# Running the softmax maxima 22 steps instead of 24 ahead of the exponentials in a fused attention block

## The chip, the core and the metric

The kernel runs on one core of one Trainium2 chip. The metric is the device time of one execution in microseconds (us); lower is better. The time quoted for a kernel is the median of its runs. A profile is taken of one more execution, and its trace gives the start and end of every instruction on the five engines: TensorE (PE, with its weight loads as PEld), VectorE (DVE), ScalarE (ACT), GpSimd (POOL) and SyncE (SP, which here only issues DMAs).

## The reference

A block with adaptive layer norms around a multi-head attention and an MLP, for 2048 rows of 512 values, 32 heads of 16 values:

```python
mod = (_silu(c) @ w_mod).reshape(c.shape[0], 6, 1, -1)
sa, ca, ga, sb, cb, gb = (mod[:, 0], mod[:, 1], mod[:, 2], mod[:, 3], mod[:, 4], mod[:, 5])
h = _layernorm(x, axis=-1) * (1 + ca) + sa
x = x + ga * _A_ref(h, A_wqkv, A_wo)        # attention
h = _layernorm(x, axis=-1) * (1 + cb) + sb
x = x + gb * _B_ref(h, B_w1, B_w2, B_w3, B_w4)  # MLP with shifted rows
# inside _A_ref:
scores = jnp.einsum("bhqd,bhkd->bhqk", q, k) * (Dh ** -0.5)
p = _softmax(scores, axis=-1)
o = jnp.einsum("bhqk,bhkd->bhqd", p, v)
```

The softmax over 2048 keys is what this change concerns. It is computed as exp(score - maximum of the row), so the maximum of each query row must be known before the first exponential of that row.

## The kernel before

**Units and steps.** Attention works through 64 units. A unit is one chunk of 512 query rows (4 chunks) times one pair of heads (16 pairs); a pair of heads lies in the two halves of the 128 partitions, `j` = 0 and 1. A unit has 16 steps, one for each tile of 128 keys, so there are 1024 steps `s`. A step has two half-steps, one for each `j`.

**What a half-step does.** Scores are computed twice, in two layouts. `score_part` (L995) computes 128 keys x 512 queries with keys on the partitions into tile `sc` (PE, L1009), and ACT takes the exponential of it into `pt` (L1005). `max_part` (L977) computes 128 queries x 512 keys into tile `mb` (PE, L993), and DVE reduces it to a row maximum `mx` (L989). `row_pair` (L1011) puts a score of step `s` and a maximum of step `s + LEAD` side by side, in different halves of the PE array, so that the two matmuls overlap. `LEAD` is the constant that the change touches; before, it is 24, one and a half units.

**From the maxima to the scores.** When the 32 maxima of a unit are done (the last is a half-step with `j` = 0), `max_fin` (L1026) finishes them: a small DVE reduce over `mx` into `mf` (L1039), two small ACT instructions (L1040, L1041), a small POOL subtraction (L1042), and then `shift_rows`, eight small DMAs on SP that write the negative maxima into two extra rows for each half of the unit's query tile `qtl` (in the trace `qtl<-nm`, 8 for a unit; all DMAs carry line L132). With those rows the score matmul subtracts the maximum by itself: it reads rows `64*j` to `64*j+63` of `qtl`, while the maximum's matmul reads only the first 62 of them. So the first score matmul of a unit with `j` = 0 has to wait until the first four of the eight DMAs have landed, and the one with `j` = 1 until all eight have.

**The rest of a step.** POOL turns each `pt` into its low half (`p_low`, L1058; now and then ACT does it, L153), and the PV matmuls (L1083, L1080) follow the exponentials by `LAG` = 2 blocks. At the end of a unit ACT copies the PV sums out (`ac`, L1100), PE turns them (`ot`, L1110), and ACT, DVE and POOL finish them (L1117, L1125, L1121).

**What sets the order.** The half-steps are taken in blocks of three, and each engine's instructions are written out in the order that a planner makes when the kernel is built; at run time every engine goes through its own list in order. The planner counts its own costs and due times (`Sched`); it holds a score back for the shift rows only by the moment they are issued, without a price for eight DMAs. All score and maximum tiles share 7 PSUM banks.

```python
blocks = [list(range(i, min(i + GRP, 2 * NS))) for i in range(-2 * LEAD, 2 * NS, GRP)]
...
        if s + LEAD < NS:
            parts.append((1 - j, max_part(s + LEAD, 1 - j)))
```

**Stages.** Before the first exponential, PE makes the maxima of the first `LEAD` steps alone, between projection matmuls. In the first quarter of attention the remaining projections (tiles `k`, `q`, `v`) are fitted between the blocks (`fill`). From then on nothing but attention runs, until the MLP begins. Loads of a unit's keys and queries are issued 32 steps ahead of its scores into one of three buffers (`load_unit`, L957), those of its values 6 steps ahead (`load_v`, L966), all on SP's one queue, in the order of the program.

Of the kernel before, what the change touches and what calls it, by code (L numbers as in the profile page):

```python
# [34 lines left out]
VMAX = 2.0 ** 14  # L35
VD = 20

LEAD = 24
LAG = 2
CARRY = 3000.0  # L40
BMAX = 1600.0
# [286 lines left out]
def kernel(ctx, tc, A_x, A_wqkv, A_wo, B_w1, B_w2, B_w3, B_w4, c, w_mod, out):  # L328
# [648 lines left out]
    def max_part(m, j):  # L977

        u, i = divmod(m, 16)
        c, g = divmod(i, 4)  # L980
        if u not in mxs:
            mxs[u] = at.tile([P, 2, 4, NC], F32, name="mx", tag="mx", bufs=2)
        x, b = bank("mb")
        ready, sm.t[x] = sm.t[x], LATE
        r = slice(64 * j, 64 * j + 62)
        lhs = qst[u][r, (g // 2) * 256:(g // 2 + 1) * 256].rearrange("p (n l) -> p l n", l=2)[:, g % 2]

        def after(e):
            end = sch.crit("D", 605, e + PX, lambda: dve.reduce_max(mxs[u][:, j, g, c:c + 1], b, axis=AX.X))  # L989
            sm.t[x] = end + XP["D"]  # L990
            if (c, g, j) == (NC - 1, 3, 0):
                max_fin(u)
        return ready, lambda: te.matmul(b, lhs, kst[u % 3][r, c * CH:(c + 1) * CH], start=True, stop=True), after  # L993

    def score_part(s, j):  # L995

        u, kt = divmod(s, NKT)
        if j == 0:
            pt[s] = at.tile([P, 2, CH], I32, name="pt", tag="pt", bufs=NPT)
        x, b = bank("sc")  # L1000
        ready, sm.t[x] = sm.t[x], LATE
        r = slice(64 * j, 64 * j + 64)

        def after(e):
            ea = sch.crit("A", 480, e + PX, lambda: act.activation(pt[s][:, j], b, AF.Exp))  # L1005
            sm.t[x] = ea + XP["A"]
            if j:
                e_exp[s] = e_hi[s] = ea
        return ready, lambda: te.matmul(b, kst[u % 3][r, kt * P:(kt + 1) * P], qst[u][r], start=True, stop=True), after  # L1009

    def row_pair(s, j):  # L1011

        parts = []
        if 0 <= s < NS:
            parts.append((j, score_part(s, j)))
        if s + LEAD < NS:
            parts.append((1 - j, max_part(s + LEAD, 1 - j)))
        parts = [x for _, x in sorted(parts, key=lambda x: x[0])]
# [575 lines left out]

    blocks = [list(range(i, min(i + GRP, 2 * NS))) for i in range(-2 * LEAD, 2 * NS, GRP)]
    pvs = [x for s in range(0, NS, 2) for x in ((s, 0), (s + 1, 0), (s, 1))]
    due = 0.0
    for k, blk in enumerate(blocks + [[]] * (LAG + CPER)):
# [18 lines left out]
        t, start = CIN, 0.0  # L1617
        need = sum((s >= 0) + (s + LEAD < NS) for s, _ in row)
        sch.flush(need)
        banks = sorted(sm.t)  # L1620
        n = 0
        for s, i in row:
            n += (s >= 0) + (s + LEAD < NS)

# [102 lines left out]
```

## Time and profile before

| | before |
|---|---|
| median of 3 runs | 2030.32 us (2027.38 to 2033.31) |
| profiled execution | 2025.04 us, of which the span is 2023.3 us |
| granted TensorE clock | 0.990 of full speed on average |
| PE / DVE / ACT / POOL busy | 1936.2 / 1658.3 / 1511.5 / 1568.8 us |
| attention's first score matmul, last score matmul | starts at 130.1 us, at 1526.1 us |

The page of the profile shows busy time over the whole span, which is a mixture: projections up to about 450 us, attention alone from there to about 1460 us, the MLP after that. Busy time of PE is modelled and counts waiting inside a pipelined matmul, so 96% there does not say that PE is at its limit. For this change the views that matter are those of the middle stage by itself, and the trace around the place where one unit's scores end and the next unit's begin.

### The profile page before, as it was taken

To read this page: it belongs to the slowest core of one execution; us is meant where nothing else is said; L and a number is where in the kernel's file an instruction comes from. 1 tells how busy PE (TensorE), PEld (TensorE's weight loads), DVE (VectorE), ACT (ScalarE), POOL (GpSimd) and SP (SyncE) were. 2 spreads that over 40 slices of the span, in tenths; PEclk is the share of its full clock that TensorE was granted. 3 is DMA by queue.
4 is the path that set the end of the run, shared out by engine and by line. 5 is a ranking of instruction groups with operands and counts; after the bars stand their busy time and mean duration, and the time that the engine had idled before them with its cause. 6 is when DMAs were issued, how large, how long until landed. Compare 5 with 4: busy or idle time off the path is not lost. (4 is left out here: it accounts for less than half of the span.)

```text
span 2023.3 us, 41663 instructions
## 1 busy us (share of the span) xinstructions
PE 1936.2 (96%) x14456; PEld 1166.2 (58%) x14456; DVE 1658.3 (82%) x2979; ACT 1511.5 (75%) x3085; POOL 1568.8 (78%) x1488
## 2 busy tenths in 40 slices
PE   8999999999999999999999999999998889999999
PEld 5755545454444444444444444444447778888998
DVE  6398788879999999999999999999965786656443
ACT  6438887768999999999999999989984554434443
POOL 6349988879999999999999999999994554425222
PEclk9989999999999999999999999999999999999999
DMA  8877666545353435353434343454414676653541
GB/s 303 234 202 184 156 187 165 133 129 124 72 107 72 107 72 107 72 107 72 101 78 92 87 93 86 93 157 100 90 38 146 233 271 262 233 184 124 189 165 68
DMA packets 185508, 278.01 MB, mean 137 GB/s; under 512 B 117104, under 2 KB 127856, under 8 KB 169008
## 3 DMA queue, kind: packets, MB, share of 16 engines
q1 hardware_dynamic: 181792, 267.20, 49.0%
q10 hardware_dynamic: 2304, 4.20, 0.6%
q0 software_dynamic: 1200, 3.93, 0.5%
q8 instruction: 115, 1.88, 0.4%
q14 instruction: 97, 0.79, 0.1%
HBM read 211.81 MB, written 62.91 MB: 136 GB/s over the span
## 5 line engine op out<-in xcount | busy, mean ns | idle before, releaser
L989 DVE TENSOR_REDUCE mx<-mb 128x1 f32<-128x512 f32 x2048 | 1250.2, 684 | 71.8 <-PE mb L993 62.7
L1058 POOL TENSOR_SCALAR pt<-pt 128x1024 f16<-128x1024 uint16 x953 | 1247.9, 1366 | 77.9 <-ACT pt L1005 74.7
L1005 ACT ACTIVATE pt<-sc 128x512 int32<-128x512 f32 x2048 | 1061.1, 615 | 122.8 <-PE mb L993 97.2
L993 PE MATMUL mb<-kst,qtl 62*128 62x512 f32 x2048 | 780.9, 461 | 21.4 <-ACT pt L1005 9.9
L1009 PE MATMUL sc<-qtl,kst 64*128 64x512 f32 x2048 | 738.7, 448 | 4.2 <-DVE mx L989 1.8
L993 PEld LDWEIGHTS mb<-kst,qtl 62*128 62x128 f32 x2048 | 359.1, 193 | 234.0 <-ACT pt L1005 160.2
L1009 PEld LDWEIGHTS sc<-qtl,kst 64*128 64x128 f32 x2048 | 335.9, 185 | 184.0 <-DVE mx L989 115.5
L1083 PE MATMUL pv<-pt,vst 128*32 128x512 f16 x4096 | 384.6, 397 | 20.6 <-ACT ac L1100 20.6
L1456 POOL TENSOR_TENSOR g<-sq,g 128x256 fp32r<-128x256 f32 (+1 forms) x124 | 98.0, 794 | 184.5 <-ACT g L1455 174.7
L1080 PE MATMUL pv<-pt,vst 128*32 128x512 f16 (+1 forms) x2048 | 221.0, 389 | 2.5 <-POOL pt L1058 2.4
L1083 PEld LDWEIGHTS <-vst 128*32 128x32 bf16 x4096 | 91.7, 93 | 226.6 <-issue 208.1
L358 PE MATMUL w<-A,wr 128*128 128x256 f32 (+1 forms) x520 | 155.6, 300 | 0.1
L356 PE MATMUL w<-A,wr 128*128 128x256 f32 (+1 forms) x520 | 155.4, 300 | 0.2 <-ACT A L350 0.2
L360 PE MATMUL w<-A,wr 128*128 128x256 f32 (+1 forms) x520 | 155.0, 299 | 0.0
L1452 ACT ACTIVATE sq<-w 128x256 f32<-128x256 f32 (+1 forms) x130 | 52.1, 402 | 123.2 <-PE w L360 113.9
L356 PE MATMUL w<-wr,g 128*128 128x512 f32 x270 | 106.7, 395 | 2.4 <-DMA wr<-Ws 2.4
L360 PE MATMUL w<-wr,g 128*128 128x512 f32 x270 | 106.2, 393 | 0.2 <-POOL g L1456 0.2
L358 PE MATMUL w<-wr,g 128*128 128x512 f32 x270 | 106.2, 393 | 0.0
L1434 DVE SCALAR_TENSOR_TENSOR sq<-sq,w 128x256 f32<-128x256 f32 (+1 forms) x130 | 58.1, 449 | 54.2 <-ACT sq L1454 53.8
L356 PEld LDWEIGHTS w<-A,wr 128*128 128x128 f32 x520 | 100.8, 194 | 1.5 <-ACT A L350 0.5
L358 PEld LDWEIGHTS w<-A,wr 128*128 128x128 f32 x520 | 100.9, 194 | 1.2 <-DVE A L346 0.4
L360 PEld LDWEIGHTS w<-A,wr 128*128 128x128 f32 x520 | 100.8, 194 | 0.5 <-issue 0.5
(156 smaller groups left out, 2124.9 us busy)
## 6 DMA issues: line engine op xcount, KB each, us to landing
wr<-Ws SPq DMA_DIRECT2D x66, 1024.0 KB, 5.9
vst<-Vs SPq DMA_DIRECT2D x64, 768.0 KB, 5.7
kst<-Ks SPq DMA_DIRECT2D x126, 384.0 KB, 6.3
Ws<-wr SPq DMA_DIRECT2D x14, 1024.0 KB, 6.3
qtl<-Qs SPq DMA_DIRECT2D x128, 96.0 KB, 4.4
Vs<-vt SPq DMA_DIRECT2D x32, 384.0 KB, 4.4
Ks<-qk SPq DMA_DIRECT2D x16, 512.0 KB, 4.0
Qs<-qk SPq DMA_DIRECT2D x16, 512.0 KB, 3.0
```

Source lines behind the costliest of these rows:

```text
L356: te.matmul(o, lh, rh, start=first, stop=False)
L358: te.matmul(o, lh, rl, start=False, stop=False)
L360: te.matmul(o, ll, rh, start=False, stop=last)
L989: end = sch.crit("D", 605, e + PX, lambda: dve.reduce_max(mxs[u][:, j, g, c:c + 1], b, axis=AX.X))
L993: return ready, lambda: te.matmul(b, lhs, kst[u % 3][r, c * CH:(c + 1) * CH], start=True, stop=True), after
L1005: ea = sch.crit("A", 480, e + PX, lambda: act.activation(pt[s][:, j], b, AF.Exp))
L1009: return ready, lambda: te.matmul(b, kst[u % 3][r, kt * P:(kt + 1) * P], qst[u][r], start=True, stop=True), after
L1058: e_low[s] = XP["G"] + sch.crit("G", 1345, ready, lambda: pool.tensor_scalar(o, i, 0.5, 1.0, op0=OP.mult, op1=OP.mult))
L1080: te.matmul(acc[r:r + n, :], v[:, kt + i, c:c + n].bitcast(F16), pt[s + i].bitcast(F16)[:, j, 0::2], start=False, stop=kt == NKT - 2, skip ...
L1083: te.matmul(acc[r:r + 32, :], v[:, kt, r:r + 32], pt[s].bitcast(F16)[:, j, 1::2], start=kt == 0, stop=False, skip_group_check=True)
L1434: dve.scalar_tensor_tensor(sq, sq, 1.0, b, op0=OP.add, op1=OP.mult)
L1456: ("G", cG(n), lambda: pool.tensor_tensor(lo, sq, hi, op=OP.subtract)), (None, 0, end), bank=b)
```

## The change

One constant. The maxima of a step are computed 22 steps ahead of its exponentials instead of 24. The computation is the same, instruction for instruction; what moves is where the maxima stand in each engine's order.

```diff
-LEAD = 24
+LEAD = 22
 LAG = 2
```

PE, at the start of attention. The first rows are projection matmuls (`k`, `q`, `vb`) with maxima `mb` of the second unit in threes between them; the excerpt ends just past the first score `sc`. Before:

```order
L993 MATMUL mb<-kst_967,qtl_965 128x512 x3
L356 MATMUL q<-hT_118,wp 128x512
L358 MATMUL q<-hT_118,wp 128x512
L360 MATMUL q<-hT_118,wp 128x512
L356 MATMUL q<-hT_118,wp 128x512
L358 MATMUL q<-hT_118,wp 128x512
L1009 MATMUL sc<-qtl_145,kst_147 128x512
L993 MATMUL mb<-kst_967,qtl_965 128x512 x2
```

And with the change, at the same place:

```order
L993 MATMUL mb<-kst_967,qtl_965 128x512 x3
L803 MATMUL vb<-wab,gcol 128x256 x3
L993 MATMUL mb<-kst_967,qtl_965 128x512 x5
L1009 MATMUL sc<-qtl_145,kst_147 128x512
L993 MATMUL mb<-kst_967,qtl_965 128x512
L356 MATMUL q<-hT_118,wp 128x512
```

Before, 48 maxima stand ahead of the first score in PE's order; now 44 do, and 4 more maxima find a score as a partner. The projections that stood there come a little later, between scores.

ACT, in the middle of attention, from one unit's L1040 (the first ACT instruction of `max_fin`) to the next unit's; L1100 is the copy of the PV sums, which stands 6 to 8 exponentials past the start of a unit's scores in both kernels. Before:

```order
L1040 ACTIVATE mf<-mf 128x8
L1041 ACTIVATE nm<-mf 128x8
L1005 ACTIVATE pt<-sc 128x512 x21
L153 ACTIVATE pt<-pt 128x1024
L1100 ACTIVATE ac<-pv 128x512
L1005 ACTIVATE pt<-sc 128x512 x6
L1117 ACTIVATE sm<-ot 128x136
L1005 ACTIVATE pt<-sc 128x512 x6
L1040 ACTIVATE mf<-mf 128x8
```

With the change, about the same unit:

```order
L1040 ACTIVATE mf<-mf 128x8
L1041 ACTIVATE nm<-mf 128x8
L1005 ACTIVATE pt<-sc 128x512 x18
L1100 ACTIVATE ac<-pv 128x512
L1005 ACTIVATE pt<-sc 128x512 x3
L153 ACTIVATE pt<-pt 128x1024
L1117 ACTIVATE sm<-ot 128x136
L1005 ACTIVATE pt<-sc 128x512 x12
L1040 ACTIVATE mf<-mf 128x8
```

L1040 stands later: fewer exponentials lie between it and L1100. Blocks of three against 32 half-steps make the place rotate over three units: the exponentials between the two are 21, 21 and 18 before, and 18, 15 and 15 now, four fewer on average, which is the two steps. On SP the order of the middle stage is the same in both kernels: the values of a unit, its eight shift rows, then the queries and keys of the unit after the next.

## The prediction

> **What bounds the kernel now.** I read the page first, then the middle stage by itself with the groups and the waits, then the place where one unit's scores give way to the next unit's. The page's busy times, of the whole span:
>
> ```profile
> span 2023.3 us, 41663 instructions
> PE 1936.2 (96%) x14456; PEld 1166.2 (58%) x14456; DVE 1658.3 (82%) x2979; ACT 1511.5 (75%) x3085; POOL 1568.8 (78%) x1488
> ```
>
> The middle stage, 524 to 1463 us: a table by windows (busy us of PE, PEld, DVE, ACT, POOL, then clock, DMA share, GB/s), the three groups that fill DVE, POOL and ACT (busy, mean ns, idle before them and who ended it), and three rows of the waits (total, times, longest):
>
> ```profile
> 524.00:1463.00 939.00, 908.01 (x7726) 430.39 (x7722) 900.02 (x1564) 867.76 (x1719) 900.43 (x767) 1.00 0.44 93
> L989 DVE TENSOR_REDUCE mx<-mb 128x1 f32<-128x512 f32 x1473 | 895.7, 684 | 32.6 <-PE mb L993 26.1 <-PE sc L1009 3.4
> L1058 POOL TENSOR_SCALAR pt<-pt 128x1024 f16<-128x1024 uint16 x676 | 879.7, 1362 | 32.3 <-ACT pt L1005 29.6
> L1005 ACT ACTIVATE pt<-sc 128x512 int32<-128x512 f32 x1473 | 760.0, 616 | 55.1 <-PE mb L993 47.2 <-PE sc L1009 1.8 <-POOL pt L1058 0.4
> DVE mx L989 <- PE mb L993: 26.1, 57, 0.8
> PE pv L1083 <- ACT ac L1100: 18.6, 16, 1.2
> PE sc L1009 <- DMA qtl<-nm: 0.2, 1, 0.2
> ```
>
> 1473 scores in 939 us are 46.0 units of 20.4 us. DVE and POOL each work 900 of the 939 us, ACT 868. A reduction costs DVE 895.7 / 1473 = 0.608 us. So the middle stage is bound by DVE and POOL together, with about 39 us (0.85 us a unit) of idle time on each. The wait of PE for the shift rows is next to nothing: 0.2 us, once. By that row alone the shift rows come in good time. How good is the question on which everything hangs, and the waits do not say it; the trace does.
>
> The matmuls are counted from the start of the span: unit u (from 0) has its last maximum as number 32u + 32 of L993, and its second score (the first with `j` = 1, which needs all eight DMAs) as number 32u + 2 of L1009. The first three rows below count L993 up to a time (units 28, 29, 30), then one just ahead of unit 29's; the next four count L1009 in the same way. Then come the eight DMA issues of the three units, and what is told of their landing for unit 29 (the extreme, 3.5, belongs to an earlier one of the eight) and for the whole stage:
>
> ```profile
> 0.00:768.80 768.80, 349.18 (x928) 161.10 (x928) 0.99 0.58 150
> 0.00:789.80 789.80, 361.65 (x960) 166.86 (x960) 0.99 0.58 148
> 0.00:810.20 810.20, 374.11 (x992) 172.46 (x992) 0.99 0.58 147
> 0.00:789.60 789.60, 361.45 (x959) 166.71 (x960) 0.99 0.58 149
> 0.00:780.00 780.00, 322.98 (x898) 149.28 (x899) 0.99 0.58 148
> 0.00:800.80 800.80, 334.79 (x929) 154.45 (x929) 0.99 0.57 147
> 0.00:800.90 800.90, 334.83 (x930) 154.51 (x930) 0.99 0.57 147
> 0.00:821.00 821.00, 346.30 (x961) 159.89 (x962) 0.99 0.57 145
> 772.35 5.29 SPq L132 DMA_DIRECT2D qtl<-nm  x8
> 793.34 5.99 SPq L132 DMA_DIRECT2D qtl<-nm  x8
> 813.74 5.00 SPq L132 DMA_DIRECT2D qtl<-nm  x8
> DMA to landing us min/median/max: 1.9/2.0/3.5
> DMA to landing us min/median/max: 1.9/2.0/4.6
> ```
>
> The last maxima start at about 768.7, 789.7 and 810.1 us, the second scores at about 780.0, 800.9 and 820.9 us: 11.1 us on average, for 18 half-steps. An issue takes some 0.6 us and its data land 2.0 us after it began, so the last of the eight lands 1.4 us after the issues end: at 779.0, 800.7 and 820.1 us. That is 10.3, 11.0 and 10.0 us after the last maximum, 10.45 on average. The slack is 0.9, 0.1 and 0.8 us. The maxima run 24 steps ahead, yet the rows arrive with half a microsecond to spare.
>
> **Part by part.** The chain behind the last maximum, unit 29. In order: DVE's rows (L1039 finishes the unit's maxima, and 22 reductions without a gap follow it), ACT's L1040, then PE around the second score (800.86):
>
> ```profile
> 787.22 1.89 DVE L989 TENSOR_REDUCE mx<-mb 128x1 f32<-128x512 f32 x3 [0.73 <-PE mb L993]
> 789.65 1.89 DVE L989 TENSOR_REDUCE mx<-mb 128x1 f32<-128x512 f32 x3 [0.55 <-PE sc L1009]
> 791.57 0.19 DVE L1039 TENSOR_REDUCE mf<-mx 128x8 f32<-128x32 f32 x1
> 791.67 13.43 DVE L989 TENSOR_REDUCE mx<-mb 128x1 f32<-128x512 f32 x22
> 792.85 0.22 ACT L1040 ACTIVATE mf<-mf 128x8 f32<-128x8 f32 x1
> 800.63 0.51 PE L993 MATMUL mb<-kst,qtl 62*128 62x512 f32 x1
> 800.86 0.47 PE L1009 MATMUL sc<-qtl,kst 64*128 64x512 f32 x1
> 801.26 0.64 PE L1083 MATMUL pv<-pt,vst 128*32 128x512 f16 x8
> 802.05 0.49 PE L1009 MATMUL sc<-qtl,kst 64*128 64x512 f32 x1
> 802.05 0.73 PE L993 MATMUL mb<-kst,qtl 62*128 62x512 f32 x2
> ```
>
> So of 11.0 us, 1.8 go by until the last maximum is reduced, 1.9 more until the first DMA is issued (the small instructions queue behind reductions, exponentials and POOL's work), 6.0 are the issues and 1.4 the last landing. The issues are the largest part, and none of it depends on `LEAD`.
>
> First, what moves. With 22 steps the last maximum of a unit stands 14 half-steps ahead of that second score, not 18. At the pace of now that is 11.1 x 14/18 = 8.6 us. The chain needs 10.45, and PE started 0.1 after the landing where it waited (unit 29), so 10.55. PE then stands at the second score of each unit for 10.55 - 8.6 = about 1.95 us. Behind it in PE's order are that unit's remaining scores, the maxima of the unit 22 steps on, and all PV groups; SP, DVE, ACT and POOL get nothing new from PE. No other matmuls are left in this stage that could stand there instead.
>
> Second, what hides it. DVE has 14 reductions to do after the unit's own last one, 14 x 0.608 = 8.5 us, and some 0.3 us of small ones; they begin 1.8 us after the last maximum and end at 10.6 us. It runs dry just when PE is released. Its next maximum then starts 0.35 us later in PE's row, or 1.2 us later where PV stands between (800.86 to 802.05 above), and takes 0.5 us. So DVE stands idle 0.85 us at least and 1.7 us at most, at a place where it had 22 reductions without a gap before. Its present idle time lies elsewhere (0.73 and 0.55 us in the rows above, ahead of the last maximum, where PE waits for the copy `ac` or does `ot`), so little of it pays for the new hole. The full 1.95 us is lost where PE cannot get ahead again, since it is held to DVE's pace by 7 shared banks. ACT has 1.5 us idle time a unit to take its share from; POOL, at 19.6 of 20.4 us, loses what its queue of finished exponentials does not cover. From below: if half of DVE's smallest hole, 0.4 us, is all that is left, and from above 2.2 us with an extra bank wait. I take 1.4, the middle of 0.85 and 1.95, since DVE decides and both its ends are equally near.
>
> Third, how often. 64 units; the first 14 lie among projections (in the order of the changed kernel projections end in unit 14), and ahead of the last one the MLP's first work already stands between. That leaves 49 boundaries: 49 x 1.4 = 69 us.
>
> Fourth, the first stage. There steps are longer:
>
> ```profile
> 160.00:460.00 300.00, 125.98 (x363) 60.38 (x363) 1.00 0.62 162
> 95.00:130.00 35.00, 33.57 (x124) 19.92 (x124) 33.37 (x59) 5.34 (x12) 8.82 (x8) 0.90 0.67 165
> 1550.00:1600.00 50.00, 40.26 (x225) 35.17 (x224) 40.72 (x87) 23.78 (x51) 27.44 (x44) 0.93 0.48 170
> ```
>
> 363 scores in 300 us (first row) make 0.83 us a half-step, 14 of them 11.6 us, more than the chain on average; where no projection falls into the 14, PE waits. Zero to 1 us for each of 14 boundaries: I take 4 us, and keep 0 and 14.
>
> Fifth, the ends. Four maxima and four scores that ran alone now share a round: four rounds fewer at 0.35 us each are -1.4 us. Ahead of the first score DVE is busy 33.4 of 35 us (second row), so two steps less there are 4 x 0.608 = 2.4 us that could come off, if PE's projections did not need the time anyway, since they only move behind the first score; I take -1 for all of it, with -4 and 0 as ends. Instructions and bytes stay the same.
>
> Sum: 69 + 4 - 1 = +72 us. The profiled execution, 2025.0 us, becomes 2097. The median of runs lies 5.3 us above it, so I forecast 2030.3 + 72, about 2102 us.
>
> **Two rules of the Trainium skill that speak about the terms.** Rows first: eight issues take 5.0, 6.0 and 5.3 us on SP, against 2.0 us for a landing. The Trainium skill, "DMA: Bandwidth & Descriptors", section "Issuing engines are not separate DMA queues", says that the sequencer's time to initiate a DMA "is usually small relative to the DMA itself". By that rule the chain would be some 5 us shorter and the change would cost nothing; the rows of this case say the opposite, and the rule counts only as the no-change rival below.
>
> **Rivals.** *No change: the slack is larger than I read.* If, with `LEAD` at 22, the small instructions pass their queues faster (1.9 us between reduction and first issue now, 1.0 if nothing stands ahead) and the four steps of `max_fin` issue without POOL's pause (5.0 instead of 5.3 to 6.0), the chain is 9.2 us. Then PE waits 0.6 us, DVE's queue covers that, and the time is 2030 us. For it speaks that the second scores of units 28 and 30 started 0.8 us after the landing, so the wait has not decided there yet. Against it speaks unit 29, with 0.1. Chance 0.07.
>
> *Faster: the ends decide.* The stall is absorbed as above, and the shorter head counts in full: -2.4 and -1.4 us, and the projections that move behind the first score fill PE where it now waits in the first stage, another 3 us or so, which gives 2023 us. The point from which it decides is a chain under 8.6 us. No unit above has one under 10.0. Chance 0.03.
>
> *Much slower: the clock falls too.* The granted clock was 1.00 in the middle stage, and 0.93 in the third row above, where PE was busy 40 of 50 us. If two idle microseconds in each unit of 22 bring the middle stage to 0.93, PE's part, not yet the bound at 20.4 us, grows by 7%, about 1.4 us a unit in which it has none to spare after the stall: 49 x 1.4 = 69 us more, 2171 us. Against it: PE's busy share in that row was 81%, and here it would remain near 90%. Chance 0.07. The Trainium skill, "TensorE: Matmul & The Clock Gate", section "HAM oscillation — how this bites in real kernels", puts the limit at gaps above about 3.4 us; a wait of 2 us would stay below it, and no run here shows one.
>
> **How the numbers follow.** Runs of this kernel differ by about 0.3%, 6 us, so less than that counts as the same. The forecast has the remaining 0.83. Its own range: 0.4 to 2.2 us at 49 boundaries, 20 to 108 us, with 0 to 14 and -4 to 0 us besides, gives 2046 to 2152 us. Two in ten outside: the no-change and the faster case (0.10 together), the clock (0.07) and a little of the forecast's tails, so 2048 to 2148 us. Slower by over 0.3%: 0.83 + 0.07 = 0.90. Within 0.3%: 0.07. Faster: 0.03.
>
> **What would show it.** Right: in the waits of the middle stage PE's scores (or their weight loads) waiting for the DMA of the shift rows go from 0.2 us to some 90 us in 40 to 50 times of about 2 us; the time from the last maximum to the landing stays at 10 to 11 us while the unit goes from 20.4 to nearly 22 us; the DVE's idle time ahead of reductions grows by 0.85 to 1.95 us a unit; the busy time of each group stays as it is, and the stage after 1500 us is only shifted. Wrong: if that wait stays below 0.5 us a unit, or if units keep 20.4 us with the wait there, or if the added time lies before 450 us or in the MLP.

## The result, and the profile after

The changed kernel takes 2134.18 us (2129.72 to 2137.81), against 2030.38 us for the kernel before on the same chip: a ratio of 1.0511, 95% interval 1.0491 to 1.0532. The forecast was 2102 us in a range of 2048 to 2148, so the sign and the range were right and 32 us were missing. The profiled execution took 2129.72 us, with a mean granted clock of 0.965 instead of 0.990.

The page's busy times, of the whole span:

```profile
span 2127.9 us, 41682 instructions
PE 1985.7 (93%) x14456; PEld 1174.7 (55%) x14456; DVE 1669.6 (78%) x2979; ACT 1534.0 (72%) x3098; POOL 1558.8 (73%) x1475
```

The same work (ACT took 13 of POOL's instructions, those of `p_low`) in 105 us more. The middle stage by windows, by groups and by waits (570 to 1560 us, one row of the windows for all of it):

```profile
570.00:1560.00 990.00, 916.59 (x7423) 421.49 (x7423) 874.60 (x1505) 849.81 (x1660) 862.57 (x730) 0.95 0.41 86
...
L989 DVE TENSOR_REDUCE mx<-mb 128x1 f32<-128x512 f32 x1417 | 871.3, 680 | 112.3 <-PE mb L993 105.3 <-PE sc L1009 5.0
L1058 POOL TENSOR_SCALAR pt<-pt 128x1024 f16<-128x1024 uint16 x642 | 841.5, 1354 | 86.3 <-ACT pt L1005 83.1 <-POOL pt L1058 0.2
L1005 ACT ACTIVATE pt<-sc 128x512 int32<-128x512 f32 x1418 | 738.0, 616 | 123.1 <-PE sc L1009 69.3 <-PE mb L993 44.4 <-POOL pt L1058 1.8
L1009 PE MATMUL sc<-qtl,kst 64*128 64x512 f32 x1416 | 533.7, 467 | 65.8 <-DMA qtl<-nm 57.6 <-DVE mx L989 7.1 <-ACT pt L1005 0.9
...
DVE mx L989 <- PE mb L993: 105.3, 150, 3.7
PE sc L1009 <- DMA qtl<-nm: 57.6, 45, 1.9
```

A reduction, a `p_low` and an exponential take as long as before (680, 1354, 616 ns). What grew is the idle time in front of them, and a row that was 0.2 us is now 57.6 us in 45 times, once per unit: PE waits for the shift rows. DVE's wait for PE's maxima follows, 105.3 us in this window of 990 us where it was 26.1 in one of 939. And the clock of this stage, 1.00 before, is 0.95.

One unit, 29 again: matmuls counted up to a time (L993 first, then L1009 twice), the eight DMA issues, and PE around the second score:

```profile
0.00:830.10 830.10, 366.31 (x960) 170.49 (x960) 0.97 0.55 141
0.00:840.90 840.90, 343.09 (x929) 160.33 (x929) 0.97 0.55 140
0.00:841.10 841.10, 343.18 (x931) 160.45 (x931) 0.97 0.55 140
...
833.72 5.75 SPq L132 DMA_DIRECT2D qtl<-nm  x8
...
838.48 0.50 PE L1009 MATMUL sc<-qtl,kst 64*128 64x512 f32 x1
838.49 0.82 PE L993 MATMUL mb<-kst,qtl 62*128 62x512 f32 x2
841.01 0.49 PE L1009 MATMUL sc<-qtl,kst 64*128 64x512 f32 x2 [1.71 <-DMA qtl<-nm]
```

The last maximum starts at about 830.0; the eight issues end at 839.47, and with 1.4 us for the last landing the rows are there at 840.9. The chain still takes 10.9 us, PE stands, and the second score starts at 841.0, as soon as the rows are there.

Where the 104.6 us of span went, by the starts of the second scores in the two traces. In the first stage (unit 0's second score to unit 15's) 13.6 us. In the middle (unit 15's to unit 62's, 47 units) 22.31 instead of 20.39 us a unit, 90.2 us. From there to the end 1.0 us. Averaged over the units from 15 on, the chain from the last maximum to the last landing takes 10.5 us (10.6 before), and the second score starts 10.6 us after that maximum (11.3 before). The hole in PE's matmul starts ahead of the second score went from 0.16 to 1.80 us.

### The profile page after: what moved, and what is told of

It reads as the page before. It is cut to its first block, busy times and chain, and to the rows that moved or that the text cites. A ratio compares the mean times of both kernels' runs of the same rounds, so it can differ in the third digit from the quotient of the medians.

```text
span 2127.9 us, 41682 instructions
## 1 busy us (share of the span) xinstructions
PE 1985.7 (93%) x14456; PEld 1174.7 (55%) x14456; DVE 1669.6 (78%) x2979; ACT 1534.0 (72%) x3098; POOL 1558.8 (73%) x1475
## 3 DMA queue, kind: packets, MB, share of 16 engines
q0 software_dynamic: 1200, 3.93, 0.5%
## 5 line engine op out<-in xcount | busy, mean ns | idle before, releaser
L1009 PE MATMUL sc<-qtl,kst 64*128 64x512 f32 x2048 | 757.3, 463 | 77.8 <-DMA qtl<-nm 64.3
L993 PE MATMUL mb<-kst,qtl 62*128 62x512 f32 x2048 | 789.9, 471 | 19.0 <-ACT pt L1005 7.2
L1009 PEld LDWEIGHTS sc<-qtl,kst 64*128 64x128 f32 x2048 | 348.8, 193 | 290.2 <-DVE mx L989 166.4
L993 PEld LDWEIGHTS mb<-kst,qtl 62*128 62x128 f32 x2048 | 366.8, 200 | 218.3 <-ACT pt L1005 144.2
L1083 PE MATMUL pv<-pt,vst 128*32 128x512 f16 x4096 | 396.3, 408 | 2.8 <-ACT ac L1100 2.8
L1080 PE MATMUL pv<-pt,vst 128*32 128x512 f16 (+1 forms) x2048 | 231.9, 400 | 2.2 <-POOL pt L1058 2.0
L153 ACT ACTIVATE pt<-pt 128x1024 f16<-128x1024 uint16 x84 | 116.7, 1389 | 0.0
L358 PEld LDWEIGHTS w<-A,wr 128*128 128x128 f32 x520 | 101.1, 194 | 1.3 <-DVE A L346 0.5
L356 PEld LDWEIGHTS w<-A,wr 128*128 128x128 f32 x520 | 100.9, 194 | 1.3 <-ACT A L350 0.5
```

The lines of the kernel that those rows point to most:

```text
L153: fn()
L356: te.matmul(o, lh, rh, start=first, stop=False)
L358: te.matmul(o, lh, rl, start=False, stop=False)
L1080: te.matmul(acc[r:r + n, :], v[:, kt + i, c:c + n].bitcast(F16), pt[s + i].bitcast(F16)[:, j, 0::2], start=False, stop=kt == NKT - 2, skip ...
L1083: te.matmul(acc[r:r + 32, :], v[:, kt, r:r + 32], pt[s].bitcast(F16)[:, j, 1::2], start=kt == 0, stop=False, skip_group_check=True)
```

## The experiments

Twelve kernels were run. The theory W: the chain from the last maximum to the landing of the eighth DMA needs 10.5 us, two steps less leave 8.6, PE waits for the rest. Rival O: a shorter look-ahead starves DVE and ACT whatever the rows do. Rival C: a good part is the TensorE clock. All numbers in one table; "first" and "unit" are the two spans defined above, "hole" the time between the starts of the second score and of the matmul before it (mean of units 15 to 62), "half" the time from unit 15 to unit 62 in which the clock records show half speed. Profiled executions, except for time and ratio. A ratio is to the kernel before as it ran in the same rounds (2027 to 2031 us); losses in us below are against that.

| kernel | time, us | ratio to before, 95% interval | first | unit | hole | half, us |
|---|---|---|---|---|---|---|
| before (24) | 2030 | 1 | 384.8 | 20.39 | 0.16 | 3 |
| after (22) | 2134.2 | 1.0511, 1.0491 to 1.0532 | 398.4 | 22.31 | 1.80 | 92 |
| e1_merge22 | 2058.9 | 1.0153, 1.0135 to 1.0172 | 400.5 | 20.64 | 0.12 | 0 |
| e5_merge24 | 2057.8 | 1.0136, 1.0114 to 1.0157 | 393.2 | 20.86 | 0.05 | 3 |
| e2_late24 | 2150.3 | 1.0602, 1.0574 to 1.0630 | 386.0 | 22.89 | 2.11 | 109 |
| e10_late24b | 2081.2 | 1.0258, 1.0239 to 1.0277 | 384.5 | 21.50 | 1.11 | 48 |
| e3_warm22 | 2109.4 | 1.0401, 1.0363 to 1.0439 | 396.9 | 21.82 | (filled) | 14 |
| e12_warm24 | 2071.4 | 1.0202, 1.0184 to 1.0221 | 389.7 | 21.24 | (filled) | 7 |
| e4_lead23 | 2103.0 | 1.0381, 1.0344 to 1.0418 | 386.3 | 21.81 | 1.03 | 65 |
| e8_lead25 | 2027.4 | 1.0001, 0.9984 to 1.0018 | 379.9 | 20.43 | 0.14 | 7 |
| e6_fix22 | 2126.7 | 1.0472, 1.0446 to 1.0498 | 392.5 | 22.31 | 1.81 | 92 |
| e7_mergefix22 | 2052.3 | 1.0107, 1.0081 to 1.0134 | 395.4 | 20.65 | 0.12 | 0 |
| e9_act22 | 2307.8 | 1.1374, 1.1342 to 1.1406 | 414.2 | 25.65 | 4.10 | 250 |
| e11_act22b | 2314.4 | 1.1393, 1.1368 to 1.1418 | 425.6 | 25.56 | 3.93 | 242 |

### Four DMAs instead of eight, at 22 and at 24

```diff
-                    for h in range(2):
-                        sch.dma(dma.dma_start,
-                                qst[u][r:r + 1, h * 256:(h + 1) * 256].bitcast(F32).rearrange("o (p l) -> o p l", l=2),
-                                nm[:, i, 4 * j + 2 * h:4 * j + 2 * h + 2].bitcast(F32))
+                    sch.dma(dma.dma_start, qst[u][r:r + 1, :].bitcast(F32).rearrange("o (p l) -> o p l", l=4),
+                            nm[:, i, 4 * j:4 * j + 4].bitcast(F32))
...
-        lhs = qst[u][r, (g // 2) * 256:(g // 2 + 1) * 256].rearrange("p (n l) -> p l n", l=2)[:, g % 2]
+        lhs = qst[u][r].rearrange("p (n l) -> p l n", l=4)[:, g]
```

The last two lines stand in `max_part`: the queries of one maximum are then every fourth one of the unit, not every second one of a half. At 22:

> LEAD 22 with four shift-row DMAs a unit instead of eight (each with 128 pieces of 16 bytes; for that a maximum takes every fourth query instead of every second of a half). Wait theory: issues shrink from 5.0-6.0 us to about 2.5 us, so the chain from the last maximum to the landing falls from 10.5 to about 8 us, under the 8.6 us that PE has; the wait goes and the time is 2030 to 2045 us. Rival (the new order itself costs, in blocks, banks or low halves, whatever the DMAs do): 2115 us or more.

At 24:

> LEAD 24 with four shift-row DMAs a unit instead of eight, the counterpart of the first experiment. Wait theory: at 24 steps the landing already came 0.7 us early on average, so little is to be had: a unit stays at 20.2 to 20.5 us and the time at 2020 to 2032 us. Rival (the middle stage before was already paced by the landing): 0.5 us a unit or more comes off, 2005 us or less.

SP's issues for one unit and the middle stage by windows, in e1_merge22:

```profile
792.14 3.38 SPq L132 DMA_DIRECT2D qtl<-nm  x4
...
570.00:1500.00 930.00, 926.45 (x7566) 522.76 (x7565) 885.92 (x1533) 859.72 (x1692) 873.40 (x743) 1.00 0.41 92
```

The issues take 2.8 us on average instead of 5.2, the chain 8.0 (at 24, 8.3) instead of 10.5. In the middle stage no wait of PE for the rows is left in either kernel (the waits of e1_merge22 have one, of 0.5 us, in the first stage), the clock is at 1.00, and 22 costs the same as 24: 2058.9 and 2057.8 us, with intervals that overlap. This is W against O: the order with 22 is as good as that with 24 as soon as the rows come in time. Two things limit it. The equal times are made up of unequal stages (22 loses 7 us to 24 in the first stage and gains 10 in the middle), and PE is busy 926 of 930 us here, so a small cost of the order could hide behind that. The next two runs test W from the other side, with the order of 24. Both kernels with four DMAs are also some 30 us slower than the one before, so both missed the times that were expected; these 30 us come with the form with four DMAs. One thing that takes longer in it is the weight load of a maximum. Before (first row) and in e5_merge24 (second), by groups of the middle stage:

```profile
L993 PEld LDWEIGHTS mb<-kst,qtl 62*128 62x128 f32 x1473 | 260.4, 192 | 168.1 <-ACT pt L1005 135.8 <-DVE mx L989 20.2
```

```profile
L993 PEld LDWEIGHTS mb<-kst,qtl 62*128 62x128 f32 x1427 | 365.6, 307 | 118.3 <-ACT pt L1005 103.6 <-DVE mx L989 8.0
L993 PE MATMUL mb<-kst,qtl 62*128 62x512 f32 x1428 | 590.2, 520 | 3.9 <-ACT pt L1005 3.8
```

Reading every fourth query as weights takes 307 ns, against 192 where every second one is read. That the 30 us come from there was not tested by itself.

### A later chain, with 24 left as it is

```diff
+scr = dr.tile([64, 4, 256], F32, name="scr")
 # in shift_rows, ahead of the rows of j = 1
+if j and u >= 15:
+    for k in range(4):                       # e10_late24b: 2
+        sch.dma(dma.dma_start, scr[u, k:k + 1, :].rearrange("o (p l) -> o p l", l=2), nm[:, 0, 0:2].bitcast(F32))
```

> LEAD 24, order of the engines as before, but from unit 15 on four more small DMAs from the same tile to an unused DRAM tile stand ahead of the last four shift rows on SP. Wait theory: the landing comes 2.4 us later, PE waits about 1.8 us at each unit's second score, and the unit grows by 1.2 us, or 2 us with clock drops: 2085 to 2130 us with no change of LEAD. Rival (the order costs, not the landing): 2030 to 2035 us.

> LEAD 24 with two extra small DMAs ahead of the last four shift rows from unit 15 on, half the dose of the second experiment. The landing comes 1.2 us later against an average slack of 0.7, so PE waits 0.4 to 0.6 us more a unit, in two of three units. If a wait costs about its own length: 2045 to 2065 us. If any wait at this place costs as much as a long one (a threshold): 2090 us or more. If waits under a microsecond are hidden: 2030 us.

SP's extra issues in the middle stage, and PE's wait over the whole span, in e2_late24:

```profile
L132 SPq DMA_DIRECT2D scr<-nm x172: 320/430/1871, 575.9 to 1541.0; - x172
...
PE sc L1009 <- DMA qtl<-nm: 63.0, 34, 3.3
```

Four more issues make the chain 13.1 us, two make it 12.1, and the kernel loses 123 and 53 us with 24 in place and the first stage as it was. The loss of the change comes back without the change. Both runs lost more than was expected; the next section says why.

### The clock

In e2_late24 and in the changed kernel the clock falls again and again for 3.4 us. One such place in the changed kernel, by windows (clock is the third number from the end). The first window holds a wait for the shift rows of 1.61 us, the second comes right behind it; the third row is the stretch of 20.55 us before:

```profile
771.52:774.93 3.41, 1.80 (x16) 0.77 (x17) 1.95 (x3) 1.68 (x3) 2.73 (x3) 1.00 0.73 145
774.93:778.34 3.41, 3.41 (x24) 1.37 (x20) 2.31 (x4) 2.57 (x5) 3.41 (x3) 0.50 0.97 148
754.38:774.93 20.55, 18.94 (x162) 8.70 (x160) 18.47 (x32) 17.52 (x35) 18.18 (x17) 1.00 0.30 70
```

All falls of a trace lie on one grid of 3.413 us. Where PE stood idle for 1.4 us or more of one cell of this grid, the next cell ran at half speed in 112 of 113 cases, over all fourteen traces of this table from 570 to 1540 us. Below 0.9 us none did; between 0.9 and 1.4 us 48 of 169 did (cells that follow one at half speed are left out, and the idle time goes by the modelled ends of matmuls). So a wait of 1.8 us makes the clock fall when it lies well inside a cell, and not when it is cut in two by a border. That is about every second unit: in the changed kernel the clock falls 25 times in the 47 units of the middle stage, twice for two cells.

```diff
 # in score_part, for the first step of a unit and j = 1, from unit 15 on
+if kt == 0 and j and u >= 15:
+    for _ in range(5):
+        te.matmul(b, kst[u % 3][r, 0:P], kst[u % 3][r, 0:CH], start=True, stop=True)
 te.matmul(b, kst[u % 3][r, kt * P:(kt + 1) * P], qst[u][r], start=True, stop=True)
```

The code is shortened; its last line is the score itself, as it was. Five matmuls whose result is overwritten fill the wait, since they need no shift rows. At 22:

> LEAD 22, and from unit 15 on five extra score-sized matmuls ahead of the first j=1 score of a unit, into that score's own bank, which it overwrites; they need no shift rows, so PE computes while it would stand still. Theory that the falling clock is a cost of its own: the 25 drops of the granted clock in the middle stage go, a unit falls from 22.3 to 21.6 us and the time to 2095-2108 us, with the wait for the rows as long as before. Rival (the low clock falls into time that is lost anyway): drops go, but 2128 to 2140 us.

The same at 24:

> LEAD 24 with the same five extra matmuls ahead of each unit's second score (units 15 to 63). It prices the extra matmuls by themselves, so that the run with them at LEAD 22 can be read. If they cost little (they fill PE's spare time of a unit), 2030 to 2045 us; then what they took back at LEAD 22 is nearly the whole cost of the fallen clock. If PE has no time for them, each unit is longer by their 2 us less what is spare, 2060 to 2110 us, and at LEAD 22 they took back correspondingly more than the difference of the two kernels shows.

The middle stage by windows, and PE's wait over the whole span, e3_warm22:

```profile
570.00:1540.00 970.00, 938.68 (x7692) 448.88 (x7691) 875.91 (x1511) 850.11 (x1666) 864.33 (x733) 0.99 0.42 88
...
PE sc L1013 <- DMA qtl<-nm: 26.2, 46, 1.8
```

And e12_warm24, with DVE's wait over the whole span (62.7 us before):

```profile
570.00:1520.00 950.00, 921.72 (x7744) 452.55 (x7745) 880.46 (x1523) 849.89 (x1670) 879.23 (x748) 1.00 0.41 89
...
DVE mx L989 <- PE mb L993: 98.2, 168, 2.1
```

With 22, more work for PE makes the kernel faster: 25 us by the medians (2134.2 to 2109.4, just above the range expected), 22 by the two ratios, give or take 9. The time from a unit's first score to its second is the same, 2.4 us in both, so the five matmuls only fill the wait; what they bring is the clock, 14 us at half speed instead of 92. With 24, where there is no wait to fill, they cost 42 us: the first score to the second takes 1.2 us instead of 0.6, and a unit 0.85 us more. So the second case of that expectation came in, but nothing is to be added to what they bring at 22, since there the matmuls stand in the wait. With them in both kernels 22 costs 38 to 40 us over 24, not 104.

How much of the loss is the clock? Some 22 to 25 us by e3_warm22, where the trace shows no other gain of the extra matmuls (its middle stage is 23 us shorter, 47 units at 21.82 instead of 22.31 us). From the changed kernel's trace by itself: 25 units that a half-speed cell touches take 22.97 us, the other 22 take 21.56, so 25 x 1.4 = 35 us. The second number may hold something else that lengthens the same units. So the wait costs 21.56 - 20.36 = 1.2 us a unit (20.36 is the kernel before, counted alike), some 56 us in 47 units, and the clock 22 to 35. The two runs with late rows at 24, counted in the same way, agree: in e2_late24 30 of the 47 units are touched and take 23.51 us, the others 21.80; in e10_late24b 14 are touched and take 22.70, the others 20.99. Without a half-speed cell a hole that grew by 1.95 us cost 1.4 us there, and one that grew by 0.95 cost 0.6.

### One step instead of two, and one more

```diff
-LEAD = 24
+LEAD = 23     # e8_lead25: 25
```

> LEAD 23: 16 half-steps between last maximum and second score. Wait theory: PE has 9.8 us for a chain of 10.5, waits 0.7 us a unit beyond the 0.1-0.2 it waits now; a unit grows by 0.3 to 0.6 us and few clock drops come: 2045 to 2065 us. Rival (cost linear in LEAD or in the order): half of 104 us, 2082 us; or no change, 2030, if it is a matter of how the blocks of three fall.

> LEAD 25, eight DMAs; projections run through without a gap and end one unit earlier. 20 half-steps between the last maximum and the second score, 12.5 us for a chain of 10.5. Wait theory: no waits for the rows are left, but the unit was bound by DVE and POOL already, so 2020 to 2032 us. Rival (time falls steadily with LEAD): 2003 us or less, 24 being on the same slope as 22 and 23.

With 23, PE's wait over the whole span, and with 25, the middle stage by windows:

```profile
PE sc L1009 <- DMA qtl<-nm: 22.8, 18, 2.3
```

```profile
524.00:1463.00 939.00, 916.23 (x7728) 437.67 (x7725) 898.16 (x1565) 866.16 (x1718) 899.97 (x767) 1.00 0.44 93
```

23 costs 76 us, nearly three quarters of what 22 costs, which was not expected: the wait comes in 18 units, not in all, since the blocks of three make the place rotate over three units; the hole is about 0.2, 0.8 and 2.0 us in turn. The unit with 2 us is long enough to bring the clock down. 25 brings nothing, 1.0001 with 0.9984 to 1.0018: DVE and POOL work 898 and 900 of 939 us there, as before. 24 lies just above the edge. A version that beats both kernels was not found.

### The gap in the first stage

In the changed kernel's order units 5 and 6 hold no projection matmuls, and the projections end in unit 14 instead of 12: loads of MLP weights (`pieces_load`) take the four staging buffers ahead of the last key weights. This makes them wait for those:

```diff
             ready[i] = yield from wt(a)
+            done.add(("w", i))
...
-        yield lambda: "rows" in done and ("vcol", 0) in done and ("vcol", 1) in done
+        yield lambda: "rows" in done and ("vcol", 0) in done and ("vcol", 1) in done and ("w", 4) in done
```

> LEAD 22, eight DMAs; only the weight pieces for the MLP are staged later, after the last key weights have got their staging buffers, so that no unit of the first stage is without projection matmuls (units 5 and 6 are in the changed kernel). Theory: the first stage gives back the 12 to 14 us that it lost, less what the shift rows cost there: 2120 to 2126 us, with the middle stage at 22.3 us a unit as it is. Rival (the first stage's loss is the wait for the shift rows too): 2130 us or more.

And with four DMAs:

> LEAD 22, four DMAs a unit, and the pieces staged later. If the wait for the rows (with the clock) and the gap in the projections are the whole loss: 2059 less 12 to 14, so 2043 to 2048 us, of which some 12 us are a slightly longer unit (20.64 against 20.39 us) and some 6 us lie in the MLP's stage. Rival (the two overlap, or the later pieces cost elsewhere): 2055 us or more.

The same 100 us of the first stage by windows, in the changed kernel and in e6_fix22:

```profile
250.00:350.00 100.00, 90.50 (x696) 43.32 (x696) 82.56 (x140) 86.72 (x170) 86.87 (x74) 0.93 0.58 141
```

```profile
250.00:350.00 100.00, 98.30 (x745) 52.24 (x743) 83.69 (x141) 84.08 (x170) 92.60 (x79) 1.00 0.65 179
```

PE's busy time and the clock of that stretch are back, and the first stage is 5.9 us shorter (5.1 with four DMAs). The medians fall by 7.5 and 6.6 us, half of what was hoped for from the first; each pair of intervals just overlaps or meets, so it is the two together, with the spans, that show it. With four DMAs, where next to nothing waits for the rows, the gain is nearly the same, so it does not hang on that wait. A gap by itself need not cost, though: with 23 units 4, 5 and 6 are without projection matmuls, and the first stage is only 1.5 us longer than before. In the changed kernel PE also waits 4.5 us for the shift rows in the first stage (0.2 before), most of it in units 4 to 7, and 24 us of that stage are at half speed (7 before); in e6_fix22 it is 2.2 and 17 us. How the 13.6 us divide between these was not found.

### Half of the rows issued by ACT

```diff
-sch.dma(dma.dma_start, ...)
+sch.dma(act.dma_start if j else dma.dma_start, ...)
 # e11_act22b besides: a unit's keys and queries 29 steps ahead
-nu, r = divmod(s + 32, 16)
+nu, r = divmod(s + 29, 16)
```

> LEAD 22, eight DMAs a unit, but the four for j=1 are issued by ACT and only the four for j=0 by SP, so that they are issued side by side; layout and weight loads as in the changed kernel. Wait theory: the chain falls from 10.5 to 8 us and the wait for the rows goes; ACT pays four issues of 0.6 us a unit, 2.4 us where it has 1.5 us idle without a stall, so a unit takes 20.8 to 21.5 us and the time is 2060 to 2095 us. If issuing costs ACT nothing: 2040 us. Rival (the order costs, not the landing): 2134 us or more.

> LEAD 22 with the rows split over SP (four) and ACT (four) as in the run before, and the key and value loads of a later unit started three of the unit's steps later, so that ACT's rows are issued before them. If ACT's rows land late because they share the DMA engines with the key loads, they land in about 2 us again (median 2.0, none of many above 4), PE's wait for the rows falls from 186.8 us to under 60, a unit takes 20.8 to 21.5 us and the kernel 2050 to 2110 us. If it is the issuing on ACT itself that delays them (ACT reaches the issue late behind its exponentials), nothing changes: landing late or not, a unit stays at 25 us and the kernel above 2250 us.

In e9_act22, units 24 and 25: what SP issued, what ACT issued, then the landing of ACT's four rows, for each unit in turn, and the second score of unit 25:

```profile
765.65 2.69 SPq L132 DMA_DIRECT2D qtl<-nm  x4
769.84 0.41 SPq L132 DMA_DIRECT2D kst<-Ks  x1
766.27 0.48 ACTq L132 DMA_DIRECT2D qtl<-nm  x1
767.49 1.43 ACTq L132 DMA_DIRECT2D qtl<-nm  x2
DMA to landing us min/median/max: 1.9/1.9/2.0
...
787.23 2.41 SPq L132 DMA_DIRECT2D qtl<-nm  x4
790.33 0.41 SPq L132 DMA_DIRECT2D kst<-Ks  x1
789.43 0.48 ACTq L132 DMA_DIRECT2D qtl<-nm  x1
790.70 1.21 ACTq L132 DMA_DIRECT2D qtl<-nm  x2
DMA to landing us min/median/max: 1.9/4.7/7.1
...
798.65 0.76 PE L1009 MATMUL sc<-qtl,kst 64*128 64x512 f32 x1 [6.77 <-DMA qtl<-nm]
```

Shorter issues made it worse by 174 us. In unit 24 ACT's rows are all issued before SP's first key load (769.84) and land in 2 us. In unit 25 ACT is held up by its exponentials, its last rows go out beside the key loads of 384 KB, and the last one lands 7.1 us after its issue; PE stands for 6.77 us. Of the units 24 to 39 every third is like 24, and the others are like 25. With all eight rows on SP, the key loads stand behind the rows in one queue and cannot get ahead. The last kernel was meant to part the two by starting the loads three steps later, but it did not: SP's loads start at the same time after the last maximum as before (7.3 to 8.2 us; they probably wait for their buffer to come free), and the result is the same. So within each trace late landing goes with key loads under way in every unit looked at (24 to 39 of both), but a kernel with the two apart was not run.

## Why the prediction was right, and where it fell short

- **The slack of half a microsecond** was right, and everything followed from it. The waits showed 0.2 us; the chain of 10.45 us against a lead of 11.1 was what told the outcome. Over the whole middle stage the slack is 0.7 us. One row was misread: up to 821.0 us it counts 961 score matmuls, so number 962, unit 30's second score, had not started at 820.9; it starts at 821.14 (the trace's row is `821.14 0.61 PE L1009 MATMUL sc<-qtl,kst 64*128 64x512 f32 x2`), and unit 30 had 1.0 us to spare instead of 0.8. After the change the chain takes 10.5 us and the second score follows 0.15 us behind the landing on average.
- **PE's wait**, forecast 1.95 us: the hole between matmul starts grew by 1.64 us, from 0.16 to 1.80. The row of the waits shows less, 57.6 us in 45 times or 1.3 us each, and not the 90 us that the forecast named, since a wait counts only from the modelled end of the matmul before. The wait was shorter because PE comes to the second score later than forecast, 9.0 us after the last maximum instead of 8.6. Half of this is the choice of units: the three that were read have a lead of 11.1 us, the whole stage 11.3, which at 14 of 18 half-steps gives 8.8. The other half is a slightly slower pace of those half-steps.
- **The cost of a wait**, forecast 1.4 us a unit between 0.85 and 1.95: 1.2 us in units without a half-speed cell. This step was right, and so was its reason: DVE runs dry at PE's release. From 1 us before the second score to 3 us after it DVE is idle 1.5 us on average, where it was 0.05 us before. e12_warm24 also shows that a delay at this place is not hidden: 0.6 us more between two scores, 0.85 us a unit.
- **The clock** is the step that failed. It stood among the rivals with 0.07, as a fall of the whole stage to 0.93 for 69 us more. It was set aside because PE's mean busy share would stay near 90%, and because the Trainium skill, "TensorE: Matmul & The Clock Gate", section "HAM oscillation — how this bites in real kernels", names idle gaps above some 3.4 us. The stage fell to 0.95 with no idle gap of PE above 1.9 us, and with PE busy 916.6 of 990 us, 93%. So the mean share did not show it; the idle time within one cell of 3.413 us did. The same page of the Trainium skill, in "Part 1: The HAM clock gate", section "What's actually happening", has the clock watched over a free-running window of 3413 ns. The length of the grid's cells in these traces bears that out; the limit of 3.4 us for a gap they do not. The missing term is 22 to 35 us. That this is also the 32 us between forecast and result is luck: the waits cost some 13 us less than forecast (56 instead of 69) and the first stage and the ends 11 us more, and these two nearly cancel.
- **The first stage**, forecast 4 us between 0 and 14: 13.6. Staging the MLP's weights later gave back 5.9 of it, by closing the projections' gap that the planner made when the order changed; the forecast did not look for that. The rest was not taken apart.
- **The ends**, forecast -1: unit 0's second score, from which the first stage is counted, starts 0.2 us sooner, and the last stage is 1.0 us longer, so +0.8.
- **No change and faster** fell with e1_merge22 and e4_lead23: 22 is free only when the chain is 8 us, and with eight issues even 23 is not. The eight issues took 5.2 us after the change too. So the sentence that the prediction quotes from the Trainium skill, "DMA: Bandwidth & Descriptors", section "Issuing engines are not separate DMA queues" (initiating is "usually small relative to the DMA itself"), has no support here: one issue took 0.59 us in the median, against 2.0 us from issue to landing, and eight of them stand one behind another.

## What to carry to other kernels

A wait of 0.2 us in the profile may have 5 us of slack or none: measure the time from the last producer to the landing and set it against the time to the consumer before shortening a look-ahead, and count the issues of small DMAs as part of that chain. When a change lets TensorE stand, price the stall and then the clock: look at the idle time in each cell of 3.4 us rather than at the mean, since in these traces 1.4 us in one cell halved the speed of the next. When a table or a constant reorders a program, look through the whole order for gaps far from the place where it acts.

## What the runs showed of the hardware that was not expected

- Half clock follows a cell of 3.413 us in which PE was idle 1.4 us or more (112 of 113 cells), so short waits cost by where they fall in the grid.
- Useless matmuls in such a wait made the kernel 22 to 25 us faster; where there was no wait they cost 42 us.
- 1 KB rows from a second queue landed up to 9.1 us after their issue beside key loads of 384 KB (2.3 us in the median of the middle stage), against 4.7 us at most and 2.0 in the median with all on one queue ahead of the loads.
- A weight load that reads every fourth value took 307 ns, every second value 192 ns.
